# A new order of all steps, and a new choice of GpSimd's, in a fused recurrent-attention and two-MLP kernel

## The chip, the core and the metric

One core of a Trainium2 chip runs the whole program. TensorE does matrix products (its granted clock has two levels, 1.2 and 2.4 GHz), VectorE and ScalarE elementwise work and reductions, GpSimd (POOL in the profile) elementwise work on SBUF only, SyncE (SP) issues all transfers. The metric is the device time of one execution in microseconds.

## The reference

Three computations in a row, on 4 batches of 768 tokens with 8 heads of 40:

```python
for t in range(S):                       # gated recurrent attention
    m_new = np.maximum(f_gate[:, :, t] + m, i_gate[:, :, t])
    f_stab = np.exp(f_gate[:, :, t] + m - m_new)
    i_stab = np.exp(i_gate[:, :, t] - m_new)
    C = f_stab * C + i_stab * (v_t outer k_t)
    n = f_stab * n + i_stab * k_t
    y[:, :, t] = sigmoid(o_t) * (C q_t) / np.maximum(np.abs(n . q_t), 1.0)
h = x @ w_in                             # first MLP, x: 3072 x 320, w_in: 320 x 1024
solu = h * softmax(h)
x = ((solu - mean) / sqrt(var + 1e-06) * g_ln) @ w_out
h = np.maximum(np.maximum(x @ w1, x @ w2), x @ w3)      # second MLP, 320 x 768 each
out = h @ w_out2
```

## The kernel before

The recurrence is computed in chunks of 128 tokens, 6 chunks for each of 4 batches, so there are 24 tiles t = 0 to 23; the second MLP works on pairs of tiles, g = 0 to 11. All products are made to near float32 precision by splitting an operand into a high part (rounded by ScalarE) and a low part (operand less high part, by VectorE or GpSimd) and adding the products of the parts.

Every piece of work is a generator that issues a few instructions and yields. The names of the generators, with the lines that the prediction touches:

- G: the gates' scans and exponentials; step Ga is a subtraction over 768 elements. B: small loads.
- L*key*: the weight loads, one transfer of 640 KB a piece (L249). D*n*: decoding of piece n (in0 is D0 and D1, in1 D2 and D3, out0 to out3 D4 to D7, m0_0 to m2_2 D8 to D16, last0 to last2 D17 to D19): ScalarE, then VectorE's L263, L264 and L266, GpSimd's addition at L270, and the split into high and low part: 512 columns at L285, the remaining columns in 64-row blocks at L298; out weights at L308.
- Q, W, V, S, I, T, Y: one attention tile. W is the decay matrix (load, GpSimd's mask at L375, for t of 8 and more a subtraction at L398 over 1,024 elements a partition, then an exponential); V loads values and keys and scales the keys (L423, 320 elements); S the scores (L434); I the part of earlier chunks (a multiplication at L449 for t under 6); T the state (a decay at L472, 336 elements); Y the output.
- X: the tile's normalization and gate (L543 to L545 on VectorE, then Xg at L547, Xm at L549 and the split Xs, 384 elements each). A: the first MLP (products L571, L620).
- U, P, F: the second MLP: products (L655), the maximum (L669) with a split of its result in three parts (L285, 512 elements), and the output product (L686).

The order is written out by hand in the string ORDER: each word names a generator and runs its next step, `*n` runs n of them, and `~z` lets the step's products be preceded by z warm-up products (L149, of a constant, their result overwritten). Each engine executes its own instructions in this order; semaphores hold an instruction until its operands and its buffer are free. SP's queue holds all transfers in the same order.

Two strings choose the engine of the elementwise steps that could run on either: a step that asks `on_pool` goes to VectorE unless POOL names it (the D splits, W, Xm, Xs), a step that asks `on_vector` goes to GpSimd unless VECTOR names it (Ga, Gb, V, I, T, Xg, P).

Of the kernel before, what the change touches and what calls it, by code (L numbers as in the profile page):

```python
# [800 lines left out]
```

## Time and profile before

| | us |
|---|---|
| runs, median of 3 (lowest, highest) | 658.84 (654.32, 661.03) |
| profiled execution, device time | 658.2 |
| its span, first to last instruction | 656.0 |
| its mean granted TensorE clock (share of 2.4 GHz) | 0.945 |
| busy TensorE, VectorE, ScalarE, GpSimd | 608.2, 511.5, 339.7, 230.3 |

Busy time is a sum over stages that differ: the weights are loaded and decoded in the first 180 us while the first attention tiles run; after that the tiles of both MLPs fill TensorE, and at the end little but products is left. The rows are to be read by stage. An engine's busy time includes time in which an instruction has begun and is held.

### The profile page before, as it was taken

How to read it: one execution, taken by the hardware profiler on the slowest of the kernel's cores; microseconds unless marked ns; L12 is line 12 of the kernel's file. 1: busy time of each engine (PE TensorE's matmuls, PEld its weight loads, DVE VectorE, ACT ScalarE, POOL GpSimd, SP SyncE). 2: the span in 40 equal slices, each digit the busy share in tenths (PEclk: the TensorE clock that was granted, in tenths of full speed). 3: DMA queues.
4: the chain of work that ended last, by engine and by line, in shares of the span. 5: the costliest groups of instructions: out<-in, count | busy, mean ns of one | idle time of the engine just before them, and what ended most of it. 6: DMA issues, size and time to landing. Idle time of an engine off the chain costs nothing.

```text
span 656.0 us, 12274 instructions
## 1 busy us (share of the span) xinstructions
PE 608.2 (93%) x4688; PEld 552.2 (84%) x4688; DVE 511.5 (78%) x860; ACT 339.7 (52%) x635; POOL 230.3 (35%) x201
## 2 busy tenths in 40 slices
...
GB/s 277 205 261 202 206 239 151 151 25 18 104 119 156 102 176 141 78 136 148 122 112 105 120 169 69 168 128 90 148 165 59 167 100 26 50 1 11 11 21 21
DMA packets 46319, 78.06 MB, mean 119 GB/s; under 512 B 5997, under 2 KB 28581, under 8 KB 46261
## 3 DMA queue, kind: packets, MB, share of 16 engines
...
## 4 chain that ended last, share of the span: by engine, by line
PE 43%; DMA 8%; DVE 6%; ACT 3%; POOL 2%; issue 2%; SPq 1%; POOLq 0%; DVEq 0%; ACTq 0%
PE pe L655 19%; PE ph L571 7%; PE po L686 6%; PE px L620 5%; DMA Wm<-rows_m 3%; DMA three<-qt 3%; PE pu L604 1%; PE py L509 1%; PE ps L431 1%; DMA xr<-ys 1%; POOL kw L423 1%; DVE tmp L669 1%; PE pi L460 1%; DVE Pr L434 1%; DMA sig<-og 1%
## 5 line engine op out<-in xcount | busy, mean ns | idle before, releaser
L655 PE MATMUL pe<-x2h,w 128*128 128x256 f32 x1080 | 167.3, 284 | 7.4 <-DVE tmp L669 7.4
L655 PEld LDWEIGHTS pe<-x2h,w 128*128 128x128 f32 x1080 | 143.5, 189 | 11.7 <-issue 5.8
L655 PE MATMUL pe<-x2l,w 128*128 128x256 f32 x648 | 111.8, 281 | 0.0
L655 PEld LDWEIGHTS pe<-x2l,w 128*128 128x128 f32 x648 | 92.0, 189 | 0.0
L285 POOL TENSOR_TENSOR h<-tmp,h 128x512 fp32r<-128x512 f32 x33 | 43.5, 1317 | 130.7 <-ACT h L283 130.7
L669 DVE TENSOR_TENSOR tmp<-pe,tmp 128x512 f32<-128x512 f32 x72 | 49.4, 686 | 48.6 <-PE pe L655 41.1
L571 PE MATMUL ph<-w,xh 128*128 128x512 f32 x240 | 71.5, 432 | 4.2 <-ACT xh L283 4.2
L686 PE MATMUL po<-w,h 128*128 128x320 f32 x432 | 67.9, 310 | 0.0
L620 PE MATMUL px<-w,uh 128*128 128x320 f32 x384 | 65.4, 312 | 0.0
L686 PEld LDWEIGHTS po<-w,h 128*128 128x128 f32 x432 | 64.1, 188 | 0.5
L620 PEld LDWEIGHTS px<-w,uh 128*128 128x128 f32 x384 | 58.9, 191 | 0.3
L571 PEld LDWEIGHTS ph<-w,xh 128*128 128x128 f32 x240 | 46.4, 208 | 13.1 <-ACT xh L283 4.6
L594 POOL TENSOR_TENSOR st<-st,nhalf 128x1 f32<-128x1 f32 x24 | 18.7, 777 | 97.9 <-DVE st L592 97.9
L375 POOL TENSOR_SCALAR_AFFINE_SELECT Wm<-Wm 128x1024 f32<-128x1024 f32 x24 | 27.8, 1159 | 66.4 <-DMA Wm<-rows_m 53.7
L509 PE MATMUL py<-Pr,V 128*42 128x128 f32 x384 | 35.4, 303 | 13.1 <-DVE Pr L434 13.1
L360 ACT CAST qst<-three 120x512 fp32r<-120x512 f32 x36 | 22.4, 622 | 47.4 <-DMA three<-qt 47.4
L578 ACT ACTIVATE e<-ph,st 128x1024 f32<-128x1024 f32 x24 | 26.8, 1115 | 35.6 <-DVE st L575 20.6
L571 PE MATMUL ph<-w,xl 128*128 128x512 f32 x144 | 42.9, 408 | 0.0
L509 PEld LDWEIGHTS py<-Pr,V 128*42 128x42 f32 x384 | 21.1, 126 | 23.1 <-DVE Pr L434 15.3
L283 ACT CAST h<-tmp 128x512 fp32r<-128x512 f32 x36 | 22.2, 618 | 35.0 <-DVE tmp L669 34.6
L270 POOL TENSOR_TENSOR stA<-stA,raw 128x640 int32<-128x640 int32 x20 | 34.7, 1735 | 13.5 <-DVE raw L266 13.3
L620 PE MATMUL px<-w,ul 128*128 128x320 f32 x192 | 36.6, 312 | 0.9 <-DVE ul L285 0.9
...
## 6 DMA issues: line engine op xcount, KB each, us to landing
...
```

The source lines that it names most:

```text
L270: pt(out=i32(A), in0=i32(A), in1=i32(low), op=ALU.add)
L283: nc.scalar.copy(out=hi, in_=x)
L285: sub(out=lo, in0=x, in1=f(hi), op=ALU.subtract)
L360: nc.scalar.copy(out=x[:, h4], in_=three[i])
L375: nc.gpsimd.affine_select(out=W, in_=W, pattern=[[0, H], [1, P]], compare_op=ALU.is_ge, fill=-NEG, base=0, channel_multiplier=-1)
L509: mm(py[half(hh, VW), i], lhsT=at[t, "V"][:, hh * 4 + i], rhs=at[t, "P", hh][:, i], start=True, stop=(qg is None))
L571: mm(out_n, lhsT=a, rhs=x, start=(i == 0), stop=(i == len(passes) - 1))
L578: nc.scalar.activation(out=e, in_=ph, func=AF.Exp, bias=s(0), accum_out=s(2))
L620: mm(px, lhsT=a, rhs=x, start=(i == 0), stop=(i == len(passes) - 1))
L655: mm(pe[:, j], lhsT=a, rhs=x, start=(i == 0), stop=(i == len(passes) - 1))
L669: tt(out=tmp, in0=pe, in1=tmp, op=ALU.max)
L686: mm(po[o], lhsT=h2[:, a, m, o * P:o * P + P], rhs=made[f"last{m // 2}"][:, 0, x * WC + m % 2 * DM:][:, 0:DM], start=(m0 == 0 and i == 0), ...
```

## The change

The ORDER string is new throughout; each generator is run for as many steps as before. Most products keep their place on TensorE to within a few. Warm-up products are asked for in twenty places (205 in all) instead of ten (132). One list POOL now names every elementwise step that GpSimd does, part by part for the splits of weights (`m0_1.0`, with an `l` behind it for the 64-row rest) and of the second MLP's maximum (`P1.0`); a step that it does not name runs on VectorE. What the steps compute, the tiles and their buffers stay. Of ORDER only the first part is shown.

```diff
-POOL = "D12 D15 D16 D17 D6 D7 D8 W2 W3 W4 W5 W6 X1m X2m X3s X4s X5s"
-VECTOR = "I1 P2 T3 V0 V3 X4g X5g"
+POOL = """
+Gb I4 P1.0 P1.2 P10.1 P11.1 P11.2 P2.1 P2.2 P3.0 P4.0 P4.1 P4.2 P5.0 P5.1 P6.1 P7.1 P7.2 P8.1 P8.2 P9.1 P9.2 T10 T15
+T16 T19 T20 T21 T22 T4 T8 V10 V13 V14 V16 V18 V19 V20 V22 V9 W10 W11 W12 W13 W14 W16 W17 W18 W20 W21 W22 W8 X10g X10m
+X10s X11m X12g X12m X12s X13s X14g X14m X14s X15g X15m X15s X16g X16m X16s X17g X17m X17s X18m X18s X19m X19s X1g X20s
+X21g X21s X22m X22s X23m X2g X2m X3g X4s X5g X5m X5s X6g X6m X7g X7m X7s X8g X8m X8s X9g X9m X9s m0_1.0 m0_2.0 m1_2.0
+m2_2.0l
+"""
 ORDER = """
-G Lin0*2 G Lin1 G~14 G*2 W0 D0 W0*2 Lin1 G D0 W0 D1 V0 G W0 D1 B G*2 D0 G B V1 G W0 D0 Q0 D1 D0 Lout0 D1 G D2 D1 G~52
-B G*2 D2 W1 V0 D3 T0~8 G D2 G*2 T0 S0.0~5 D2 V1 S0.1 S0.0 D1 Lout1 D2 D3 D1 Q1 S0.1 Y0 D1 D3 Lout2 D1*2 D3 D4 W1 G I1
-D1 Y0 Lout3 D3 W1 Y0 D4 S1.0~7 D4 W1 D1 Y0 D1 O0 D3 D4 D5 S1.1 T1 S1.0 D5 I1 V2 D4 T1 W2 S1.1 Y1 T1 D4 D3*2 X0 D3*2 W3
-D3 D6 D3 D5 O0 Lm0_0 D3 V2 D4 T2*2 X0 Y1 V3 X0 Y1 D6 Y1 T2 W2 I2 D7 X0 Q2 D5 W3 X0 D7 X0 Lm0_1 A0~10 D6 W2 D8 D6 D8
-Lm0_2 V3 W3 W2 D7 A0 D7 X1 D8 I2 W3 S2.0 Lm1_0 A0 S2.1 Lm1_1 D5 S2.0 A0 S2.1 Y2~9 X1*2 Q3 D5 D6 W4 A0 Y2 T3*2 Y2 X1 I3
-D5 A0 V4 D7 T3 Y2 X1 A0 D6 Lm1_2 X1 A1~20 A0 D6 A0 D7 A0 W4 D9 Lm2_0 S3.0 D7 D9 I3 S3.1 D10 S3.0 A0 X2 D10 S3.1 A0
-Lm2_1 D8 D11 Y3 V4 D9 A0 D11 W4 A0 Q4 A0 D9 A1 Y3 I4 Y3 A0 T4 V5 W4 X2 Y3 X2 T4 W5 A0 D8 T4 A1 O1 X2 D8 D10 I4 Lm2_2
-X2 A1 S4.0 X2 D10 S4.1 A0 A1 X3 A0 D8*2 Q5 A0 S4.0 A2~2 A1 A0 D8 Llast0 S4.1 O1 D9 A1 A2 D11 W6 W5 A1 X3 Y4 D9 A1
-Llast1 D12 X3 A1 D12 A2 W5 A1 Y4 I5 A1 Y4 S5.0 V6 A1 X3 A1*2 D10 S5.1 Y4 X3 A1 Llast2 W5 A1 D9 X3 D11 D12 D9 D10 S5.0
-A2 S5.1 X4 I5 Y5 D9 W7 A1 A2 D13*2 D10 D11 A2 Q6 A2 D12 D10 A2 X4 A2 D11 V7 D12 A1 Y5 I7 A2 Y5 A3 A1 Y5 V6 D10 D12 A1
-W6 D14 D11 D14 X4 D11 D13 Q6 T6 A2 T6 A2 X5 X4 U0 T6 T7 D11 A2 T6*2 D13 D15 A2 D12 A2 T6 U0 P0 A2 D15 D14 D12 A2 P0
-D14 D12 D15 D13 D17 D15 D17 Q6 A3 D14 A2 D17 D13 Q6 D13*2 A2 D14 U0 A3 A2 X4*2 A2 A3 U0 P0 W6 D13 P0 A3 D16 U0 D16 D14
...
+G Lin0*2 Lout0 G G~12 W0 G*5 G~5 G*2 D0*3 D1 Lin1 W0*2 G G~13 G*3 Q0 S0.1~12 W0 W1 G*2 D0 B D1*3 D2 V0 Lout1 D4 W0*2
+S0.1 G D0 D2*2 B D1 V0 T0~25 D2 T0 V1 D1 Lin1 W1 D1*4 D3*2 S0.0*2 Q1 Y0~10 D2 D1*3 I1 D4 D3*2 W1*2 Lout3 V1 V2 T1 B Y0
+S1.1*2 Lout2 D3 S1.0*2 Y0*2 D4*2 V2 O0 D4 D3 X0 D6 T1~6 T1 W3 Lm0_0 I1 Q2 Y1~7 D3*7 D4*2 W2 D5*2 S2.1~16 D5 Lm0_2 I2
+D5 T2 O0 Lm0_1 D6 X0 D7 W3 V3 X0 Y1*3 W2 D7 T2*2 X0*2 D8*2 D6*2 I2 W2*2 D8 S2.0 W3*2 X0 A0~11 Q3 A0 X1 D7*2 S2.1 Lm1_0
+D5*2 S2.0 Y2*3 V3 A0*2 D6 W4 S3.1 X1*2 V4 D5 D10*2 I3 Y2 X2 D8 T3*2 D6 X1 D7 S3.0 A0*2 I3 D7 Lm2_1 W4 A0*3 S3.0 Lm1_1
+X1*2 A1~25 W4 Q4 A1 D8 S3.1 W5 T3 D6 D9*2 D7 D8 A0 A0~5 A0 D9 X2*2 D12 Y3 D8*2 V6 D8 A0*5 W4 X2 D11*2 O1 X2 W5 I4 Y3*3
+X3 A1*2 S4.0 V4 X2 A0 D9 T4*2 D10*2 O1 S4.1 Lm1_2 A0*2 D9 S4.0 I4 Q5 A1*2 A2~10 A2 A1 D9 T4 S4.1 W6 Y4 I5 X3*2 A1*2 A0
+X3*2 A1*3 D11 V5 X3 D12 A2 Y4 A1 Lm2_0 A1*3 A1~4 Llast2 Y4*2 X4 D9*2 W5*2 D12 D9 D13 S5.0 D13 D11 D10*2 I5 A2 Llast1
+D12*3 S5.0 S5.1*2 Y5~6 I7 W7 D11 A2*3 A3 X4 A1*2 D10*2 A2 D13 A3 X4 V6 Llast0 D10 X4 A1*2 T6 D14*2 A2*2 D12*3 A2~7 A2
+V7 Y5 D15 W6 T6*3 T7 T6 D11*2 D13 D15 D14 U0*2 P0 A2*5 D13*2 D15 Lm2_2 U0 D14 D11*2 A2 V7 D14 P0 U0 D17 D15 D17*2 T6
+Y5 P0 U0~5 Q6 X4*2 D13*2 A3 Q6*9 A3 A2 S6.0 A2 P0 D15 W6 Y5 D14 A3*2 D13 D16*2 D17 D14 A4~9 A4 P0*2 D14 A2 D17 A3*3
...
-    def on_pool(name):
+    def pick(name):
-    def on_vector(name):
-        return tt if name in VECTOR.split() else pt
-        on_vector("Ga")(out=gr, in0=gi, in1=Mend.to_broadcast([BH, NC, P]), op=ALU.subtract)
+        pick("Ga")(out=gr, in0=gi, in1=Mend.to_broadcast([BH, NC, P]), op=ALU.subtract)
-        on_vector("Gb")(out=gf, in0=mp.unsqueeze(2).to_broadcast([BH, NC, P]), in1=gM, op=ALU.subtract)
+        pick("Gb")(out=gf, in0=mp.unsqueeze(2).to_broadcast([BH, NC, P]), in1=gM, op=ALU.subtract)
-    def decode(key, i, n, sub):
+    def decode(key, i, n, name):
-            yield from split_weight(key, halves[key, j], w[:, j], sub)
+            yield from split_weight(key, halves[key, j], w[:, j], f"{key}.{j}")
-    def split(hi, lo, x, sub):
+    def split(hi, lo, x, name):
-        sub(out=lo, in0=x, in1=f(hi), op=ALU.subtract)
-    def split_weight(key, A, w, sub):
+        pick(name)(out=lo, in0=x, in1=f(hi), op=ALU.subtract)
+    def split_weight(key, A, w, name):
-            yield from split(w[:, 0:512], w[:, 512:1024], A[:, 0:512], sub)
+            yield from split(w[:, 0:512], w[:, 512:1024], A[:, 0:512], name)
-                sub(out=w[low, to], in0=A[high, 512:640], in1=f(w[high, to]), op=ALU.subtract)
+                pick(name + "l")(out=w[low, to], in0=A[high, 512:640], in1=f(w[high, to]), op=ALU.subtract)
-            yield from split(w[:, 0:WC], w[:, WC:2 * WC], A, sub)
+            yield from split(w[:, 0:WC], w[:, WC:2 * WC], A, name)
-                on_pool(f"W{t}")(out=W, in0=W, in1=a_t, op=ALU.subtract)
+                pick(f"W{t}")(out=W, in0=W, in1=a_t, op=ALU.subtract)
-            on_vector(f"V{t}")(out=kw, in0=kw, in1=wT[:, c, b * H:(b + 1) * H].unsqueeze(2).to_broadcast([P, H, D]), op=ALU.mult)
+            pick(f"V{t}")(out=kw, in0=kw, in1=wT[:, c, b * H:(b + 1) * H].unsqueeze(2).to_broadcast([P, H, D]), op=ALU.mult)
-            on_vector(f"I{t}")(out=q, in0=q, in1=at[t, "qk"][0], op=ALU.mult)
+            pick(f"I{t}")(out=q, in0=q, in1=at[t, "qk"][0], op=ALU.mult)
-            on_vector(f"T{t}")(out=C, in0=Cs[t], in1=decb[:, b * H:(b + 1) * H, c:c + 1].to_broadcast([D, H, VW]), op=ALU.mult)
+            pick(f"T{t}")(out=C, in0=Cs[t], in1=decb[:, b * H:(b + 1) * H, c:c + 1].to_broadcast([D, H, VW]), op=ALU.mult)
-        on_vector(f"X{t}g")(out=xr, in0=xr, in1=sig[t // 3][:, t % 3], op=ALU.mult)
-        on_pool(f"X{t}m")(out=xr, in0=xr, in1=nq.unsqueeze(1).to_broadcast([P, 3, P]), op=ALU.mult)
+        pick(f"X{t}g")(out=xr, in0=xr, in1=sig[t // 3][:, t % 3], op=ALU.mult)
+        pick(f"X{t}m")(out=xr, in0=xr, in1=nq.unsqueeze(1).to_broadcast([P, 3, P]), op=ALU.mult)
-        yield from split(xh, xl, xr, on_pool(f"X{t}s"))
+        yield from split(xh, xl, xr, f"X{t}s")
-            yield from split(uh[:, sl], ul[:, sl], pu, tt)
+            yield from split(uh[:, sl], ul[:, sl], pu, "")
-        yield from split(x2t[g2][0][:, :, sl], x2t[g2][1][:, :, sl], pq, tt)
+        yield from split(x2t[g2][0][:, :, sl], x2t[g2][1][:, :, sl], pq, "")
-            yield from split(h2[:, 0, ms2], h2[:, 1, ms2], tmp, on_vector(f"P{g}"))
+            yield from split(h2[:, 0, ms2], h2[:, 1, ms2], tmp, f"P{g}.{m}")
-            procs[name] = decode(key, i, len(src), on_pool(name))
+            procs[name] = decode(key, i, len(src), name)
```

## Rows read from the trace of the kernel before

**Rows 1.** Busy us (count) by window: PE, PEld, DVE, ACT, POOL; granted clock, DMA, GB/s
```profile
0.00:60.00 60.00, 45.75 (x293) 35.24 (x293) 55.37 (x76) 37.28 (x72) 29.56 (x26) 0.72 0.76 249
60.00:120.00 60.00, 49.04 (x333) 33.60 (x334) 52.70 (x88) 38.64 (x77) 31.24 (x24) 0.80 0.62 190
120.00:180.00 60.00, 50.90 (x366) 45.74 (x366) 58.55 (x85) 43.47 (x88) 38.68 (x34) 0.91 0.21 63
180.00:240.00 60.00, 55.99 (x445) 52.64 (x444) 52.76 (x92) 27.91 (x54) 23.62 (x19) 0.97 0.50 144
240.00:540.00 300.00, 293.76 (x2395) 275.81 (x2394) 245.00 (x432) 157.37 (x280) 88.67 (x82) 1.00 0.43 123
540.00:656.00 116.00, 112.75 (x865) 109.15 (x863) 47.12 (x92) 35.03 (x69) 18.48 (x17) 1.00 0.06 20
```

**Rows 2.** Timeline at 42 us: VectorE, then GpSimd (start, length in us)
```profile
42.31 3.90 DVE L543 SCALAR_TENSOR_TENSOR nq<-nq 128x128 f32<-128x128 f32 x1
42.25 0.76 POOL L472 TENSOR_TENSOR C<-C,decb 40x336 f32<-40x336 f32 x1 [4.64 <-PE py L512]
42.97 1.01 POOL L547 TENSOR_TENSOR xr<-xr,sig 128x384 f32<-128x384 f32 x1
43.92 2.14 POOL L375 TENSOR_SCALAR_AFFINE_SELECT Wm<-Wm 128x1024 f32<-128x1024 f32 x2
```

**Rows 3.** Lines of VectorE in the first 180 us (busy us, mean ns)
```profile
L264 DVE TENSOR_SCALAR stA<-stA 128x640 int32<-128x640 int32 x20 | 21.3, 1065 | 0.7
L266 DVE SCALAR_TENSOR_TENSOR raw<-raw 128x640 int32<-128x640 int32 x20 | 21.7, 1083 | 0.1
L543 DVE SCALAR_TENSOR_TENSOR nq<-nq 128x128 f32<-128x128 f32 x6 | 8.1, 1351 | 0.0
L298 DVE TENSOR_TENSOR w<-stA,w 64x128 fp32r<-64x128 f32 x18 | 10.3, 571 | 0.8 <-ACT w L295 0.3
L423 DVE TENSOR_TENSOR kw<-kw,wT 128x320 f32<-128x320 f32 x2 | 4.8, 2421 | 0.0
```

**Rows 4.** The same lines' durations, ns: shortest, median, longest (first 180 us)
```profile
L264 DVE TENSOR_SCALAR stA<-stA x20: 493/882/1773, 11.2 to 172.9; 128x640 int32<-128x640 int32 x20
L266 DVE SCALAR_TENSOR_TENSOR raw<-raw x20: 808/816/3015, 12.8 to 174.1; 128x640 int32<-128x640 int32 x20
L543 DVE SCALAR_TENSOR_TENSOR nq<-nq x6: 280/364/3898, 42.3 to 160.6; 128x128 f32<-128x128 f32 x6
L298 DVE TENSOR_TENSOR w<-stA,w x18: 284/288/1621, 26.5 to 154.0; 64x128 fp32r<-64x128 f32 x18
L423 DVE TENSOR_TENSOR kw<-kw,wT x2: 473/2421/4369, 16.6 to 53.6; 128x320 f32<-128x320 f32 x2
```

**Rows 5.** Prices by line of moved steps; last row: shortest, median, longest
```profile
L285 POOL TENSOR_TENSOR h<-tmp,h 128x512 fp32r<-128x512 f32 x33 | 43.5, 1317 | 130.7 <-ACT h L283 130.7
L285 POOL TENSOR_TENSOR xl<-xr,xh 128x384 fp32r<-128x384 f32 x3 | 3.1, 1037 | 8.3 <-DMA gb<-rows_g 5.3 <-ACT xh L283 3.0
L449 POOL TENSOR_TENSOR gb<-gb,q 40x1024 f32<-40x1024 f32 x4 | 10.7, 2663 | 4.3 <-DMA q<-qt 4.3
L398 DVE TENSOR_TENSOR Wm<-Wm,aT 128x1024 f32<-128x1024 f32 x16 | 19.5, 1216 | 15.6 <-POOL Wm L375 15.6
L285 DVE TENSOR_TENSOR h<-tmp,h 128x512 fp32r<-128x512 f32 x3 | 2.1, 688 | 0.0
L285 DVE TENSOR_TENSOR xl<-xr,xh 128x384 fp32r<-128x384 f32 x21 | 11.6, 554 | 3.2 <-ACT xh L283 3.2
L423 POOL TENSOR_TENSOR kw<-kw,wT x6: 722/1112/1307, 20.5 to 176.5; 128x320 f32<-128x320 f32 x6
```

**Rows 6.** Timeline at 224 us: GpSimd, and TensorE behind it
```profile
224.71 3.89 POOL L423 TENSOR_TENSOR kw<-kw,wT 128x320 f32<-128x320 f32 x1
228.65 0.51 PE L480 MATMUL pc<-V,kw 128*40 128x42 f32 x16 [3.17 <-POOL kw L423]
```

**Rows 7.** Timeline of TensorE at 42 us: ten warm-up products
```profile
42.76 2.31 PE L149 MATMUL ph<-ident 128*128 128x256 bf16 x10
```

More of the change, by code (lines that the diff above doesn't have):

```diff
@@ new lines @@
+A5*2 D19 P0 U1 Q7 D18*2 V8 T8 P0*2 D19*2 F0 Q7*5 Y6 T8 T9 O2 A4*2 X6 A4*2 F0 X6 I7*2 Q7*3 A4*3 F0*3 P1 A4 Q7 X6*4 W8
+I7 T8 I7 A4*2 F0 P1 S7.0 T8*3 A5*2 S7.0 S7.1*2 Q8 A5 U1 W9 A4*3 W8*2 P1 A5*5 Y7 V9 P1*2 Y7 U1 P1 U1*2 P1 Q8*4 I8 A5*2
+V9 Q8*3 W9 U1 W8 Y7*2 X7 T9 A5*3 T9 S8.0 Q8*2 A5 T10 A5 P1 S8.0 W9 S8.1*2 P1*3 X7 I8*4 Q9 T9*4 U1*2 P1 A5*4 Q9*9 Y8
+V10 Y8 V10 P1 I9 U2 A6*3 X7*4 W10*2 A6 U2 Y8*2 X8 P1*2 I9*4 T10*6 A6*3 F1*2 A6*3 W9 S9.1*2 S9.0*2 Q10 A7*2 X8 W11 F1
+W10 A6*5 W10 Y9*2 V12 Q10 A6*2 X8*4 A7 V12 A7*2 F1 A6*2 Q10*8 I10 A8 F1 W11 P2 S10.0*2 W11 A7*3 I10 P2 O3*2 U2 Y9
```

74 lines of the change are left out of this document (29 added, 45 removed).

## The prediction

> **What bounds the kernel now.** I read the busy times by stage first [rows 1]. From 240 to 540 us TensorE is busy 293.8 of 300 us at its upper clock level (2.4 GHz, granted clock 1.00), and from 540 to 656 us 112.8 of 116: there TensorE's own work sets the time, and a reader should see that little is left to win, 6.2 us of idle in the long middle. The first 180 us are another kernel: TensorE is busy 45.8, 49.0 and 50.9 of 60 us, its granted clock is 0.72, 0.80 and 0.91 (so 33.6 + 24 + 10.8 = 68 us at the lower level, 1.2 GHz), and VectorE is busy 55.4 + 52.7 + 58.6 = 166.6 of 180 us. VectorE bounds this stage; it idles only 13.4 us.
>
> Is that VectorE work or waiting? I went to the timeline of a place where a VectorE step was slow [rows 2]. A step of L543, 128x128, took 3.90 us; GpSimd ran four steps back to back from 42.25 to 46.06 us, and the VectorE step ended 0.15 us after the last. So a "busy" VectorE can be one that is held while GpSimd works. Setting the mean of a line in the first 180 us [rows 3] against the shortest of the same instruction [rows 4] gives what was lost: L264 20 x (1.065 - 0.493) = 11.4, L266 20 x (1.083 - 0.808) = 5.5, L543 6 x (1.351 - 0.280) = 6.4, L298 18 x (0.571 - 0.284) = 5.2, L423 2 x (2.421 - 0.473) = 3.9: 32.4 us in five lines, a floor. GpSimd was busy 29.6 + 31.2 + 38.7 = 99.5 us meanwhile [rows 1], so each us of GpSimd cost VectorE about 0.33 us.
>
> It goes the other way too. At 224.71 us a GpSimd step of L423 took 3.89 us (0.722 undisturbed [rows 5]) and TensorE sat 3.17 us waiting for it [rows 6]; the granted clock of 180 to 240 us is 0.97 [rows 1].
>
> **The change, part by part.** (a) *VectorE's own work in the first stage, up to the last product of U1.* From GpSimd to VectorE come four weight splits of 512 (m0_0, m1_1, m2_1, m2_2) at 0.688, one of 640 at 0.86, six 64-row rests at 0.284, Ga at 0.75 of 1.216, I2, I3 and I5 at 1.216 (VectorE's price for 1,024 elements a partition), V1, V2, V4, V6, V7, V8 and T1, T2, T7 at 0.473 (336 elements against V's 320), P0's three and P1.1 at 0.688, X0g, X1m and X3s at 0.554: 2.75 + 0.86 + 1.70 + 0.91 + 3.65 + 4.26 + 2.75 + 1.66 = 18.5 us. From VectorE go three splits (m0_1, m0_2, m1_2), five X steps and W8: 2.06 + 2.77 + 1.22 = 6.1 us. Net **+12.5 us** [rows 4, 5]. Counting at the same prices all VectorE steps listed ahead of U2's first product in both orders gives +12.8, so the order itself moves little there.
>
> (b) *What GpSimd no longer holds.* The same steps at GpSimd's prices (1.317 a split or P, 2.663 an I, 0.722 a V or T, 1.037 an X [rows 5]; rests and Ga at the same ratio of 1.9) take 34.7 us away, and 3 x 1.317 + 5 x 1.037 + 2.63 (W8) = 11.8 come: GpSimd falls by 22.9 us, from 99.5 to 76.6. In proportion VectorE gets back 22.9 x 0.33 = 7.6 us. But the long losses came from runs of steps [rows 2], and a run shortens in length as well as in number: with the square of the load the loss of 32.4 falls by 1 - (76.6/99.5)^2 = 41%, **-13.4 us**. I take this, as the row at 42 us is nearest to it. The ends are 0 and -22.9 (every us given back). So (a) and (b) together are -0.9: moving the steps is nearly free in this stage, neither the gain nor the loss that the counts alone suggest.
>
> The Trainium skill, page "SBUF — State Buffer", section "SBUF: two separate sides", says the port pair that VectorE and GpSimd share is an exclusive lock held for the whole instruction. Read so, a VectorE step would wait for one GpSimd instruction at most; the row at 42 us shows four waited out, 3.9 us against 0.28, so here the measurement goes further than the page. By the page's rule (b) would be the proportional -7.6 and the sum below 656.2.
>
> (c) *Warm-up products and the clock.* The order asks for 205 instead of 132, in twenty places instead of ten. Raising 68 us of lower level helps only where TensorE was what VectorE waited for, and VectorE idles 13.4 us in the whole stage [rows 1]: ends 0 and -13.4, I take **-6**, since the waits are shared with ScalarE and the loads. (d) *Their price.* Of the 73 additional ones 22 stand ahead of A2, where TensorE waits anyway (five at U11 go), and 56 from A2's first product on; ten of 256 columns took 2.31 us at the lower level [rows 7], so 0.23 each there and half of it at the upper: 6.5 to 12.9 us. TensorE's idle time from 60 to 180 us, 11.0 + 9.1 [rows 1], hides most; I take **+4**, with ends 0 and 12.9 where the cover is gone.
>
> (e) *The stall at 224 us.* V8 goes to VectorE, where it takes its turn: **-3** of the 3.17 us [rows 6]; ends 0 and -5, with the clock regained (0.03 of 60 us is 1.8 us). What is late next is the chain through L362 on VectorE that held it.
>
> (f) *From U2 on.* Eleven W subtractions, 27 X steps and two P splits leave VectorE (13.4 + 15.0 + 1.4), eleven P, seven Xg, six V and T come (7.6 + 3.9 + 2.8): -15.4 us. GpSimd gets 28.9 + 28.0 + 2.6 and gives 26.1: +33.4 us. A W step has no GpSimd row; the nearest are I's 2.663 (as many elements) and twice a split, 2.63. VectorE is not the bound here, so of the 6.2 us idle TensorE I take **-2**; ends -6 and the first rival.
>
> (g) *Loads.* The order shifts SP's queue: the second piece of in1 waits behind B, V0, V1 and the gate rows; V6 stands ahead of V5; Lm2_2 is last of the weights. VectorE, 55.4 of 60 us busy, covers this: 0. Uncovered, one 640 KB load at the 249 GB/s of 0 to 60 us is 2.6 us [rows 1].
>
> **Sum:** 12.5 - 13.4 - 6 + 4 - 3 - 2 = -7.9 us, against the profiled execution's 658.2 us (span 656.0 and 2.2 around it): **650.3 us**. The runs shown have a median of 658.84, so this is 1.3% faster.
>
> **The rivals.** *GpSimd's runs reach into the steady stage (slower).* A mask (1.07 us [rows 2]) and now its subtraction of 2.63 on the same engine are a run of 3.7 us, and three X steps one of 3.1; a VectorE step that meets them waits, with the max steps and score products that feed TensorE queued behind. VectorE has 55 us idle in 240 to 540 [rows 1], thirteen tokens, 4.2 us a token, 5.2 with the relief of (f). Held longer than 5.2 us a token, the rest falls on TensorE: both runs in full are 6.8, 1.6 us over, 12 times 19 us: 650.3 + 2 + 19 = **671**. Against it: nearly all of the 33 P splits on GpSimd [rows 5] run after 180 us already, and TensorE still idles only 2%.
>
> *The change does little (no change).* Losses fall only in proportion (12.5 - 7.6), the clock gives nothing because VectorE was never waiting for it, the products cost 4, the stall goes, (f) is nothing: +5.9, less 3: **661**. For it: VectorE idle is small; against it: run lengths.
>
> *All shared waiting goes (much faster).* (b) at -22.9, (c) at -11, (d) +2, (e) -5, (f) -4: 12.5 - 40.9 = -28.4: **630**. For it: 32.4 is a floor; against it: the load of GpSimd is still 77 us.
>
> **How the numbers follow.** My forecast 0.38, with its own range 641 to 660; no change 0.26; much faster 0.18; slower 0.18. About 1% is what a measurement of this kernel can tell from no change, so faster is below 652. Of my forecast five eighths lie there (0.24), and with the much faster case and a little of the second rival that is 0.44; the rest of my forecast (0.14) and 0.20 of the second give same 0.34; the slower case and the tail of the second 0.22. The range 632 to 670 leaves out half of the two outer cases, 0.18.
>
> **What would show it.** In the changed profile's first 180 us: mean of L264 from 1.07 to about 0.8 us and GpSimd near 77 us busy (b); granted clock above 0.72, 0.80 and 0.91 (c); the same TensorE work reached some 5 us sooner; no wait of TensorE for L423 near 220 us (e); TensorE idle at most 6 us in 240 to 540 (f). I am wrong if L264 and L543 are as slow as before, if VectorE's steps lengthen beside the W subtractions, or if TensorE waits for xh or for a weight.

## The result, and the profile after

The changed kernel takes 661.73 us (656.73 to 665.76), beside 656.23 us for the kernel before on the same chip: a ratio of 1.0077, 95% interval 1.0051 to 1.0103. It is 0.8% slower, where 1.3% faster was forecast. Its profiled execution takes 664.41 us with a span of 662.6. Lines of the changed kernel have numbers lower by 7 (L264 is L257, L655 is L648).

The stages of after, one row a window (PE, PEld, DVE, ACT, POOL busy us; granted clock, DMA share, GB/s), as [rows 1]:

```profile
0.00:60.00 60.00, 49.87 (x311) 36.90 (x313) 53.69 (x87) 37.86 (x74) 24.86 (x20) 0.81 0.80 248
60.00:120.00 60.00, 51.80 (x404) 37.87 (x405) 55.13 (x101) 40.80 (x80) 22.92 (x18) 0.91 0.55 175
120.00:180.00 60.00, 50.29 (x387) 46.05 (x386) 56.58 (x94) 40.82 (x85) 25.72 (x21) 0.97 0.26 84
180.00:240.00 60.00, 58.03 (x472) 54.08 (x471) 50.98 (x84) 31.36 (x60) 28.35 (x25) 1.00 0.50 153
240.00:540.00 300.00, 284.79 (x2297) 268.54 (x2295) 228.49 (x401) 147.19 (x263) 101.94 (x97) 0.98 0.39 117
540.00:663.00 123.00, 118.51 (x905) 114.79 (x903) 55.21 (x104) 38.89 (x78) 16.08 (x16) 0.99 0.09 28
```

The first 180 us look as forecast in GpSimd, busy 24.9 + 22.9 + 25.7 = 73.5 us (99.5 before), and in the clock of the second and third window (0.91 and 0.97 for 0.80 and 0.91). The first window's 0.81 for 0.72 is no rise. The profile counts time ahead of the trace's first clock record as the upper level; that record stands at 23.0 us in after and at 11.0 in before. TensorE's products ran at the lower level ahead of it, as the score products of after show, first up to 22 us, then from 95 to 160 us, where the granted clock is 1.00 (mean ns):

```profile
L424 PE MATMUL ps<-q,k 40*128 40x128 f32 x8 | 2.1, 437 | 0.7 <-DMA q<-qt 0.7
L424 PE MATMUL ps<-q,k 40*128 40x128 f32 x16 | 2.0, 278 | 0.0
```

With the unrecorded time counted as lower level the first window has 0.61 in after and 0.62 in before. What is new is the long middle: TensorE idles 15.2 us of 300 from 240 to 540 us, 6.2 before, and its clock is no longer 1.00.

The same stretch, all that TensorE waited for (total us, times, longest us), first of after:

```profile
PE ps L424 <- DVE kst L355: 6.9, 3, 3.6
PE ph L564 <- DVE u L576: 2.3, 2, 1.6
PE pq L625 <- ACT x L616: 2.3, 1, 2.3
PE po L679 <- DVE Pr L427: 1.6, 1, 1.6
PE pe L648 <- DVE tmp L662: 1.2, 1, 1.2
PE pu L597 <- DVE u L589: 0.8, 1, 0.8
```

and of before, where no wait is over 1.2 us:

```profile
PE pq L632 <- ACT x L623: 2.8, 4, 1.1
PE pe L655 <- DVE tmp L669: 2.6, 4, 1.2
PE ps L431 <- DVE kst L362: 0.5, 1, 0.5
PE pc L480 <- POOL kw L423: 0.4, 2, 0.2
```

After has nine waits where before has eleven, but they sum to 15.1 us (6.3 before), 12.8 of it for VectorE. The longest one in after's timeline (start, length; idle time before it and its cause in brackets):

```profile
398.44 5.97 DVE L355 SCALAR_TENSOR_TENSOR qst<-qst,part,three 120x512 fp32r<-120x512 f32 x1
397.84 0.90 POOL L491 TENSOR_TENSOR Cl<-C,cst 40x336 fp32r<-40x336 f32 x1
398.71 1.09 POOL L368 TENSOR_SCALAR_AFFINE_SELECT Wm<-Wm 128x1024 f32<-128x1024 f32 x1
399.76 1.30 POOL L278 TENSOR_TENSOR h<-tmp,h 128x512 fp32r<-128x512 f32 x1
401.02 1.89 POOL L391 TENSOR_TENSOR Wm<-Wm,aT 128x1024 f32<-128x1024 f32 x1
402.88 0.98 POOL L542 TENSOR_TENSOR xr<-xr,nq 128x384 f32<-128x384 f32 x1
404.34 0.74 DVE L355 SCALAR_TENSOR_TENSOR kst<-kst,part,three 120x512 fp32r<-120x512 f32 x1
405.13 1.00 PE L424 MATMUL ps<-qst,kst 120*128 120x128 f32 x4 [3.57 <-DVE kst L355]
```

GpSimd ran five steps back to back from 397.84 to 403.86 us: a mask and its subtraction, with a split and an X step between and behind. A VectorE step took 5.97 us beside them, until 0.55 us after the last; the next of the same kind took 0.74. (L355, L362 before, makes the two operands of the scores.) The step behind it was late for the scores, and TensorE sat 3.57 us. The granted clock behind this wait, behind the one at 378 us and behind a third that ended at 478.36 us (1.98 us long), in windows:

```profile
378.00:382.00 4.00, 4.00 (x20) 4.00 (x20) 3.96 (x8) 2.10 (x4) 0.20 (x1) 0.58 0.40 86
405.00:409.00 4.00, 3.87 (x14) 3.35 (x15) 2.56 (x5) 0.97 (x2) 0.00 (x0) 0.57 0.39 123
480.00:484.00 4.00, 4.00 (x19) 4.00 (x20) 1.40 (x4) 0.97 (x2) 0.00 (x0) 0.57 0.42 129
```

A mean near 0.58 is mostly the lower level (1.2 GHz). In each of these three windows that is 0.42 or 0.43 of 4 us, so some 1.7 us of lost work on top of the wait.

Where the time goes is told by TensorE's progress: the first product of a pair of tiles g in the second MLP, us later (+) or sooner (-) than in before, worked out from the traces of the runs below:

```
                              U0     U2     U4     U5     U6     U8    last
after                       -4.9   -7.9   -5.1   -4.4   +3.7   +6.1   +6.5
b_choicea (old order)       -8.8   -6.9   -9.4   -9.9  -10.7   -6.0   -6.0
ba_newc (new order from U2) -7.3   -5.3   -4.4   -3.7   -0.3   +5.7   +6.6
ab_newc (new order to U2)   -8.4   -5.8   -4.5   -3.8   -4.1   +1.7   +1.7
a_lessp                     -2.1   -5.1   -4.7   -5.1   -4.8   -3.9   -3.4
```

After is 7.9 us ahead at U2 (211 us) and loses 14.4 us from there to the end. Some 5 us of that lead are no gain: sixteen products of the first MLP and four score products that before makes ahead of U2 stand behind it in after (16 x 0.30 + 4 x 0.14 us, the mean busy time of one in before). At U4 both have made the same products, and there after is 5.1 us ahead. From U4 to the end (after, then before):

```profile
311.00:659.30 348.30, 335.22 (x2641) 319.16 (x2639) 228.35 (x407) 150.28 (x276) 92.65 (x90) 0.99 0.29 86
316.10:652.80 336.70, 331.74 (x2645) 314.68 (x2643) 230.71 (x415) 148.53 (x275) 87.75 (x82) 1.00 0.31 90
```

After takes 11.6 us longer here: TensorE idles 13.1 us instead of 5.0, and three times 1.7 us go to the lower clock. Of the loss 8.1 us fall between U5 and U6: that is 359 to 413 us, where the waits at 378 and 405 us lie. One caution: runs that share all their code up to U2 differ there by up to 8 us, so single entries are to be read to a few us, and verdicts rest on the ratios.

### The profile page after: what moved, and what is told of

The parts are those of the page before. It is cut to its first block, busy times and chain, and to the rows that moved or that the text cites. A ratio compares the mean times of both kernels' runs of the same rounds, so it can differ in the third digit from the quotient of the medians.

```text
span 662.6 us, 12377 instructions
## 1 busy us (share of the span) xinstructions
PE 613.3 (93%) x4761; PEld 558.2 (84%) x4761; DVE 500.1 (75%) x866; ACT 336.9 (51%) x635; POOL 219.9 (33%) x195
## 4 chain that ended last, share of the span: by engine, by line
PE 55%; DVE 22%; DMA 9%; ACT 6%; issue 4%; SPq 2%; POOL 0%; ACTq 0%; DVEq 0%; POOLq 0%
PE pe L648 22%; PE ph L564 10%; PE po L679 6%; PE px L613 6%; DMA three<-kt 3%; PE ps L424 2%; DMA three<-qt 2%; PE py L502 2%; PE pu L597 2%; DMA q<-qt 2%; DVE u L576 2%; DVE kst L355 2%; DVE st L567 2%; DVE raw L259 1%; ACT e L571 1%
## 5 line engine op out<-in xcount | busy, mean ns | idle before, releaser
L648 PE MATMUL pe<-x2h,w 128*128 128x256 f32 x1080 | 166.7, 284 | 4.5 <-DVE tmp L662 3.0
L648 PEld LDWEIGHTS pe<-x2h,w 128*128 128x128 f32 x1080 | 143.8, 189 | 7.8 <-issue 2.7
L648 PE MATMUL pe<-x2l,w 128*128 128x256 f32 x648 | 111.4, 280 | 0.0
L648 PEld LDWEIGHTS pe<-x2l,w 128*128 128x128 f32 x648 | 91.7, 188 | 0.0
L679 PE MATMUL po<-w,h 128*128 128x320 f32 x432 | 70.3, 317 | 1.6 <-DVE Pr L427 1.6
L564 PE MATMUL ph<-w,xh 128*128 128x512 f32 x240 | 67.7, 413 | 3.8 <-DVE u L576 3.8
L679 PEld LDWEIGHTS po<-w,h 128*128 128x128 f32 x432 | 66.1, 194 | 2.4 <-DVE Pr L427 1.8
L564 PEld LDWEIGHTS ph<-w,xh 128*128 128x128 f32 x240 | 44.5, 197 | 13.3 <-DVE u L576 2.9
L278 POOL TENSOR_TENSOR h<-tmp,h 128x512 fp32r<-128x512 f32 x20 | 27.4, 1368 | 78.6 <-ACT h L276 65.7
L355 DVE SCALAR_TENSOR_TENSOR qst<-qst,part,three 120x512 fp32r<-120x512 f32 x36 | 37.6, 1044 | 15.3 <-ACT qst L353 12.2
L276 ACT CAST uh<-pu 128x512 fp32r<-128x512 f32 x48 | 26.0, 588 | 35.2 <-PE pu L597 35.1
L587 POOL TENSOR_TENSOR st<-st,nhalf 128x1 f32<-128x1 f32 x24 | 14.2, 594 | 87.3 <-DVE st L585 87.2
L567 DVE TENSOR_REDUCE st<-ph 128x1 f32<-128x512 f32 x48 | 30.7, 681 | 15.7 <-PE ph L564 15.7
L142 PEld LDWEIGHTS <-ident 128*128 128x128 bf16 x205 | 24.3, 127 | 17.1 <-issue 9.3
```

Source lines behind the costliest of these rows:

```text
L276: nc.scalar.copy(out=hi, in_=x)
L278: pick(name)(out=lo, in0=x, in1=f(hi), op=ALU.subtract)
L355: nc.vector.scalar_tensor_tensor(out=x[:, h4], in0=f(x[:, h4]), scalar=part[:, i:i + 1], in1=three[i], op0=ALU.mult, op1=ALU.add)
L564: mm(out_n, lhsT=a, rhs=x, start=(i == 0), stop=(i == len(passes) - 1))
L567: nc.vector.tensor_reduce(out=s(n), in_=ph[:, n * 512:(n + 1) * 512], axis=AX.X, op=ALU.max, negate=True)
L648: mm(pe[:, j], lhsT=a, rhs=x, start=(i == 0), stop=(i == len(passes) - 1))
```

## The experiments

Theory 1: the gain is lost again by the late choice, GpSimd's runs of mask and subtraction above all (the prediction's slower rival). Theory 2: it is lost by the order itself, which the prediction counted at nothing. Ratios are to the kernel before of the same call, with their 95% interval.

### Choice of engines, and order

**b_choicea**: the new choice, in the order and with the warm-ups of before.

```diff
-POOL = "D12 D15 D16 D17 D6 D7 D8 W2 W3 W4 W5 W6 X1m X2m X3s X4s X5s"
-VECTOR = "I1 P2 T3 V0 V3 X4g X5g"
+POOL = """
+Gb I4 P1.0 P1.2 P10.1 P11.1 P11.2 P2.1 P2.2 P3.0 P4.0 P4.1 P4.2 P5.0 P5.1 P6.1 P7.1 P7.2 P8.1 P8.2 P9.1 P9.2 T10 T15
...
```

> The order and the warm-ups of before; only the choice of engines is the changed one, everywhere. Theory 1: the late runs cost as much as in the changed kernel (about +12) and the early relief gives some of its 6 to 8 us: 658 to 668 us, with L362 (the same step as L355) held for several us at least once. Theory 2: the choice alone does no harm, 650 to 657 us.

Measured: 650.27 us, 0.9857 (0.9811 to 0.9902): faster than both kernels. Its first three windows, its middle, and its L264 (here L269):

```profile
0.00:60.00 60.00, 46.61 (x317) 35.01 (x317) 55.47 (x93) 39.34 (x76) 24.57 (x20) 0.74 0.78 256
60.00:120.00 60.00, 51.00 (x372) 38.73 (x369) 55.76 (x99) 43.10 (x85) 24.68 (x19) 0.83 0.66 200
120.00:180.00 60.00, 47.66 (x352) 43.06 (x351) 58.97 (x93) 40.79 (x82) 29.32 (x23) 0.97 0.20 60
240.00:540.00 300.00, 290.86 (x2353) 272.71 (x2352) 234.79 (x404) 147.66 (x266) 111.34 (x98) 0.99 0.42 121
L269 DVE TENSOR_SCALAR stA<-stA 128x640 int32<-128x640 int32 x20 | 16.0, 798 | 0.7
```

GpSimd is busy 78.6 us in the first 180 (76.6 forecast) and the mean of L264 is 0.80 us (about 0.8 forecast). In the middle GpSimd does 111.3 us, more than in after, and TensorE idles only 9.1. So the late choice does no harm that this measurement can tell in the order of before.

**splice_u2, ab_newc, ba_newc**: one order ahead of U2's first product, the other behind it. splice_u2 has the order, warm-ups and choice of after, then those of before; ab_newc the same with the new choice throughout; ba_newc the new choice throughout, the order of before, then that of after.

```diff
 ORDER = """
-G Lin0*2 Lout0 G G~12 W0 G*5 G~5 G*2 D0*3 D1 Lin1 W0*2 G G~13 G*3 Q0 S0.1~12 W0 W1 G*2 D0 B D1*3 D2 V0 Lout1 D4 W0*2
+G Lin0*2 G Lin1 G~14 G*2 W0 D0 W0*2 Lin1 G D0 W0 D1 V0 G W0 D1 B G*2 D0 G B V1 G W0 D0 Q0 D1 D0 Lout0 D1 G D2 D1 G~52
...
```

This is the beginning of ba_newc's order against that of after; behind U2's first product its words stand as in after. In ab_newc and splice_u2 it is the other way round.

> The changed kernel's order, warm-ups and choice up to U2's first product, then the order and the choice of before for what is left. Theories 1 and 2 alike: 648 to 651 us, because U2 starts at 211.4 us instead of 219.3 and what follows is as before. Theory 3 (the early gain is only borrowed: steps were put off, and the late stage pays for them whatever its order): 655 to 658 us.

> The changed choice of engines everywhere; the changed order and its warm-ups up to U2's first product, then the order of before. Theory A (the choice gains about 8 us in the first 120 us, the changed order of the late steps loses about 12 between 300 and 510 us): 649 to 654 us, with TensorE busy 290 or more of 300 us from 240 to 540 us. Theory B (the changed order already harms in the early stage, by leaving later work unprepared): 657 to 662 us.

> The changed choice of engines everywhere; the order and warm-ups of before up to U2's first product, then the changed order. Theory A: 659 to 664 us, the loss of the late order in full, TensorE busy about 285 of 300 us from 240 to 540 us. Theory B: 649 to 654 us.

Measured: splice_u2 1.0009 (0.9984 to 1.0034); ab_newc 0.9995 (0.9963 to 1.0027); ba_newc 1.0118 (1.0078 to 1.0158). All three have the good choice ahead of U2, and none keeps b_choicea's gain: the new order costs 1.4% where it stands early (with its warm-ups) and 2.6% where it stands late. The two don't add: after, with both, is 2.2% behind b_choicea. For splice_u2 (659.25 us) theories 1 and 2 both missed, and theory 3 came nearest; ab_newc (657.88) is where theory B had it; ba_newc (665.75) went past theory A's 664. So both parts of the new order cost. Theories 3 and B both say that its early part puts steps off which are paid for later. The progress table fits that: ab_newc is 5.8 us ahead at U2, b_choicea 6.9, with the same products made and the same order behind, and by U4 they are 4.9 us apart, 7.7 at the end. It doesn't prove it, as the seam between two orders that were not made for each other may cost something as well.

**b_to_u6**: as ba_newc, but the order changes at U6. Against b_choicea it differs only from there on:

```diff
 ORDER = """
...
-P5 S17.1 Y16 S17.0 P5 A14 U6 P5 V18 S17.1 A14*2 W19 U6 Y16 A14 Y16 A14 Y16 A14 V18 I17 A15 I17 W19 T18 X16 I17 T18 A14
...
```

> The new choice of engines with the order and warm-ups of before up to U6's first product, then the order of after. The same with the change of order at U2 was 1.0118, and the order of before to the end 0.9857. If the late order loses place by place (in the profiles two thirds of the loss are made by U6): 0.989 to 0.995. If it is lost after U6 or at the joint, wherever it stands: 1.003 to 1.012.

Measured: 0.9892 (0.9831 to 0.9953). The late order's loss is made on the way, most of it ahead of U6; from U6 on the new order and the seam there cost together 0.35%, which is within the noise of the two runs.

### Which part of the choice

**b_attn**: the kernel before with only I2, I3, I5, V1, V2, V4, V6, V7, V8, T1 and T2 moved to VectorE. Its list against the list that says the same as before's two strings:

```diff
-V1 V2 V4 V6 V7 V8 V9 V10 V12 V13 V14 V15 V16 V18 V19 V20 V21 V22 I2 I3 I4 I5 T1 T2 T4 T7 T8 T9 T10 ...
+V9 V10 V12 V13 V14 V15 V16 V18 V19 V20 V21 V22 I4 T4 T7 T8 T9 T10 ...
```

**b_early_newc**: b_choicea with the choice of before from U2 on. **a_lateb**: after, likewise with the choice of before from U2 on (W8 stays on GpSimd in both, the other W go to VectorE). Their lists begin

```diff
-Gb I4 P1.0 P1.2 P10.1 P11.1 P11.2 P2.1 P2.2 P3.0 P4.0 P4.1 P4.2 P5.0 P5.1 P6.1 P7.1 P7.2 P8.1 P8.2 P9.1 P9.2 T10 T15
+m0_1.0 m0_2.0 m1_2.0 m2_2.0l Gb X1g X2g X2m X3g I4 T4 X4s X5g X5m X5s X6g X6m X7g X7m X7s W8 T8 X8g V9 X9g V10 T10
...
```

(b_early_newc; a_lateb has no X7m and X7s.)

> The kernel before with eleven early attention steps alone moved from GpSimd to VectorE: I2, I3, I5, V1, V2, V4, V6, V7, V8, T1, T2. By the prediction's prices VectorE's own work grows by 3.65 + 8 x 0.473 = 7.4 us and GpSimd's falls by 8.0 + 8 x 0.722 = 13.8. Theory P (long GpSimd steps hold VectorE for longer than VectorE itself needs for them): 649 to 654 us, most of the gain of the whole choice (8.5 us), and the mean of L264 from 1.07 to 0.9 us or less. Theory Q (the gain comes from the weight splits and the late steps): 656 to 662 us.

> The order and warm-ups of before; the changed choice of engines for the steps ahead of U2's first product only, the choice of before for later ones. Theory A (the gain of the choice is made in the first 120 us): 648 to 652 us, and the W subtractions on GpSimd are worth nothing in this order. Theory C (the late choice matters, VectorE's relief in the steady stage): 653 to 658 us.

> The changed order and warm-ups; the changed choice of engines for all steps ahead of U2's first product, the choice of before for all later ones. Theory 1 (runs on GpSimd in the steady stage): 649 to 654 us, since the early gain of 6 to 8 us stays and the late loss goes. Theory 2 (order): 660 to 664 us. If only W matters within theory 1, this and the kernel with W alone put back are alike within 2 us.

Measured: b_attn 0.9936 (0.9912 to 0.996), about half the gain from eleven steps; b_early_newc 0.9888 (0.9843 to 0.9933), nearly all of it; a_lateb 1.0425 (1.038 to 1.047). The same late choice is worth 0.3% in the old order, within the noise, and 3.5% in the new one. Theory 1 as first put falls: without the late choice the new order is far worse. Theory 2 (as changed, 660 to 664 us) missed a_lateb's 687.33 us as well. In b_attn the other sign that was expected, a mean of L264 of 0.9 us or less, did not come (it is L268 there; 1.07 us before):

```profile
L268 DVE TENSOR_SCALAR stA<-stA 128x640 int32<-128x640 int32 x20 | 23.0, 1148 | 0.7
```

The mean of one line does not tell the gain; VectorE's busy time up to U2 does better (the rows under (a) and (b) below).

### Warm-ups

**b_newc_warm**: b_choicea with the 205 warm-ups at after's steps. **b_newc_nowarm**: b_choicea with none. **a_oldwarm**: after with the 132 of before.

```diff
-G Lin0*2 Lout0 G G~12 W0 G*5 G~5 G*2 D0*3 D1 Lin1 W0*2 G G~13 G*3 Q0 S0.1~12 W0 W1 G*2 D0 B D1*3 D2 V0 Lout1 D4 W0*2
+G Lin0*2 Lout0 G G~14 W0 G*8 D0*3 D1 Lin1 W0*2 G G~52 G*3 Q0 S0.1 W0 W1 G*2 D0 B D1*3 D2 V0 Lout1 D4 W0*2 S0.1 G D0
...
```

This is a_oldwarm against after: only the `~z` differ, the steps stay. In the same way b_newc_warm asks for `G~12` where b_choicea has `G~14`, and b_newc_nowarm has no `~z` at all.

> The order of before with the changed choice of engines (650.3 us with the warm-ups of before), and the changed kernel's 205 warm-up products ahead of the same steps as there. If the warm-ups do nothing where VectorE bounds the stage: 648 to 652 us, with a higher granted clock in the first 180 us. If they gain: 643 to 647 us. If they cost TensorE time: 653 to 657 us.

> The order of before with the changed choice, and no warm-up product at all. If warm-ups only cost where VectorE bounds the stage: 646 to 650 us, at a lower granted clock in the first 120 us. If the 132 of before are worth having: 653 to 660 us.

> The changed order and choice with the 132 warm-up products of before, ahead of the same steps as there, in place of the 205. If the additional warm-ups cost what they cost in the order of before (5 us): 655 to 659 us. If they are worth their time here, where the granted clock of the first 180 us rose to 0.81, 0.91 and 0.97: 663 to 668 us.

Measured: b_newc_warm 0.9943 (0.9904 to 0.9981), b_newc_nowarm 0.9887 (0.9845 to 0.9928), a_oldwarm 1.0152 (1.0109 to 1.0195). In the old order the 73 additional products cost 0.9% and none at all does as well as 132 within the noise (651.96 us, between the two ranges that were expected); in the new order the 73 are worth 0.7%. b_newc_nowarm's first windows, and then b_newc_warm's:

```profile
0.00:60.00 60.00, 33.14 (x202) 24.64 (x204) 55.41 (x93) 39.42 (x76) 24.58 (x20) 0.98 0.79 256
60.00:120.00 60.00, 53.57 (x329) 38.34 (x328) 48.06 (x90) 39.96 (x79) 23.28 (x18) 0.70 0.64 194
0.00:60.00 60.00, 44.58 (x305) 34.62 (x305) 56.39 (x88) 37.72 (x73) 24.39 (x20) 0.83 0.77 251
60.00:120.00 60.00, 51.12 (x400) 37.22 (x401) 55.25 (x96) 42.20 (x84) 23.24 (x18) 0.89 0.66 199
```

The 0.98 of b_newc_nowarm is again time without a clock record, here up to 50.7 us. Its output products of attention, up to 50 us and from 99 to 112 us (granted clock 1.00), show the lower level:

```profile
L513 PE MATMUL py<-Pr,V 128*42 128x128 f32 x32 | 5.8, 425 | 3.5 <-DVE Pr L438 3.5
L513 PE MATMUL py<-Pr,V 128*42 128x128 f32 x32 | 3.4, 289 | 0.0
```

With that time counted as lower level the first window has 0.56 without warm-ups, 0.64 with 132 (b_choicea) and 0.69 with 205, and the second 0.70, 0.83 and 0.89. The clock rises with the number of warm-ups, and the time doesn't follow: none and 132 end within 0.3% of each other, and 205 is the slowest (its profiled execution, 662.07 us, is one of its longest). So a higher clock in the first stage is not by itself worth its price.

### Why VectorE is late in the new order

**a_wvec**: after, with the twelve W subtractions that it has on GpSimd back on VectorE. **a_repair**: after, with six products that waited moved one or two TensorE steps later (one of the six places is shown).

```diff
-T16 T19 T20 T21 T22 T4 T8 V10 V13 V14 V16 V18 V19 V20 V22 V9 W10 W11 W12 W13 W14 W16 W17 W18 W20 W21 W22 W8 X10g X10m
+T16 T19 T20 T21 T22 T4 T8 V10 V13 V14 V16 V18 V19 V20 V22 V9 X10g X10m X10s X11m X12g X12m X12s X13s X14g X14m X14s
...
```

```diff
-Q11 P2*2 U2 Q11*5 S11.0 Q11*3 A7*2 P2*3 U2 W11 S11.0
+Q11 P2*2 U2 Q11*8 A7*2 P2*3 U2 S11.0 W11 S11.0
...
```

> The changed kernel with one thing put back: the twelve W subtractions (L391, 1.90 us each on GpSimd, 1.22 on VectorE) run on VectorE again; order, warm-ups and all other choices as changed. Theory 1 (runs: at 398.44 us a step of L355 took 5.97 us instead of 0.75 because GpSimd ran Cl, mask, P, W and Xm back to back; such runs in the steady stage hold VectorE and then TensorE): most of the 12 us lost between 300 and 510 us come back, 651 to 656 us, mean of L355 from 1.04 and 0.85 back to about 0.8 us. Theory 2 (order: the new order of the late steps loses the time, whichever engine does them): 660 to 664 us, as changed.

> The changed kernel with six places of its late order mended and nothing else: products that TensorE began by waiting for VectorE (S11.0, A10's first, A12's first, S17.0, A14's transposes, S20.0; waits of 1.31, 1.60, 0.71, 3.57, 0.77 and 1.98 us, 9.9 together) stand one or two TensorE steps later, so that TensorE does ready work while VectorE finishes. Theory O (the late order sets products too close behind the VectorE steps that they wait for): 652 to 657 us, with TensorE busy about 291 of 300 us from 240 to 540 us. Theory V (VectorE itself is too late in this order, so the waits only move to the next product): 659 to 664 us.

Measured: a_wvec 1.0178 (1.0134 to 1.0223), worse by 1.0% than after, which both theories missed (671.78 us). a_repair 1.0073 (1.005 to 1.0097), no change. Its waits from 240 to 540 us begin with

```profile
PE pc L473 <- POOL kw L416: 4.4, 2, 3.6
PE pq L625 <- ACT x L616: 2.8, 2, 2.5
PE ps L424 <- DVE kst L355: 2.3, 3, 1.0
```

The total is no less, 14.4 us beside 15.1: it moved from the scores to the state's products. So the loss does not lie in the place of these six products. A guess that remains is that VectorE and GpSimd have no room in this order. The next runs take work away, in either order.

**a_lessv, b_lessv** leave out two VectorE steps a tile (tiles 8 to 23, 16 x 1.22 = 19.5 us), in after and in b_choicea; **a_lessp, b_lessp** leave out the W subtractions of tiles 9 to 23; **a_lessvp** both, in after. The expectations of the W runs take all fifteen subtractions for GpSimd's. In the new choice only eleven of them are (11 x 1.9 = 21 us); W9, W15, W19 and W23 are VectorE's (4 x 1.22 = 4.9 us) and go too.

```diff
-        ts(out=nq, in0=nq, scalar1=1.0, scalar2=None, op0=ALU.max)
-        nc.vector.reciprocal(out=nq, in_=nq)
+        if t < 8:
+            ts(out=nq, in0=nq, scalar1=1.0, scalar2=None, op0=ALU.max)
+            nc.vector.reciprocal(out=nq, in_=nq)
```

```diff
-                pick(f"W{t}")(out=W, in0=W, in1=a_t, op=ALU.subtract)
+                if t == NA:
+                    pick(f"W{t}")(out=W, in0=W, in1=a_t, op=ALU.subtract)
```

> The kernel after, with two of VectorE's own steps (the maximum and the reciprocal of nq, 0.42 and 0.95 us) left out for tokens 8 to 23, so the scores are not normed there: 16 x 1.37 = 22 us less VectorE work in the steady stage. The kernel after is at 1.0077. Theory V (in the late part of the new order VectorE's own load makes its results late for TensorE): at least half of the 12 us comes back, 0.988 to 0.997. Theory H (VectorE is late because runs of GpSimd steps hold it): little, 1.001 to 1.008. Theory P (TensorE's products stand too close whatever the others do): 1.005 to 1.010.

> The new choice of engines in the order and with the warm-ups of before (0.9857), with the same two VectorE steps left out for tokens 8 to 23 as in a_lessv: 22 us less VectorE work. Theory V says that VectorE is late only in the new order's steps: 0.982 to 0.987, a gain of at most 0.4%. If less VectorE work helps here as much as in the new order (0.970 to 0.980), its load says nothing of the order.

> The kernel after, with GpSimd's W subtractions left out for tokens 9 to 23 (the decay is not subtracted there): 15 x 1.9 = 28 us less GpSimd work in the steady stage, no VectorE step less. Theory H: the runs of mask and W are halved, at least half of the 12 us comes back, 0.988 to 0.997. Theory V: GpSimd's share is small, 1.002 to 1.008. Theory P: 1.005 to 1.010.

> The new choice of engines in the order and with the warm-ups of before (0.9857), with GpSimd's W subtractions left out for tokens 9 to 23 as in a_lessp (there 28 us less GpSimd work gave 1.2%). If the order of before has room for these steps, as it had for the 22 us of VectorE work left out in b_lessv (0.9859): 0.982 to 0.987. If runs of GpSimd steps hold VectorE in either order at the same price, the new order is not what makes them dear: 0.970 to 0.977.

> The kernel after with both left out: the two VectorE steps of a_lessv (alone 0.9977) and the W subtractions of a_lessp (alone 0.9953); after itself is at 1.0077. If both act on the same waits (VectorE's room in the steady stage, whichever engine fills it), the second adds little: 0.990 to 0.996. If they act on separate waits, the gains add: 0.983 to 0.988. In either case it should not go below the order of before with the same left out (about 0.985).

Measured:

| left out | in after (1.0077) | in b_choicea (0.9857) |
|---|---|---|
| VectorE's two steps | 0.9977 (0.9943 to 1.0011) | 0.9859 (0.9804 to 0.9914) |
| W subtractions (eleven GpSimd, four VectorE) | 0.9953 (0.9911 to 0.9995) | 0.9874 (0.9841 to 0.9907) |
| both | 0.9949 (0.9921 to 0.9977) | |

In the old order neither gives anything that can be told from noise. In the new order each gives about 1%, and both together no more than the better one alone, as expected if the two act on the same waits. a_lessp is where theory H had it and theory V had not; a_lessv lies just outside V's range and outside H's; theory P missed both. The W runs are no clean test of GpSimd, because of the four VectorE steps: at a_lessv's rate (1.0% for 19.5 us) these would be worth 0.25% of the 1.2%. In a_lessv's one profile (659.75 us, its median is 655.90) the late loss is still there (the kernel is 13.0 us ahead at U2 and 1.9 behind at the end), so only its ratio speaks for it. a_lessp's profile fits the mechanism; its middle, and the VectorE steps that were held at 398 us in after:

```profile
240.00:540.00 300.00, 291.78 (x2379) 275.29 (x2378) 225.32 (x407) 153.07 (x275) 87.38 (x89) 1.00 0.41 122
395.27 0.99 DVE L355 SCALAR_TENSOR_TENSOR qst<-qst,part,three 120x512 fp32r<-120x512 f32 x1
396.56 1.41 DVE L355 SCALAR_TENSOR_TENSOR kst<-kst,part,three 120x512 fp32r<-120x512 f32 x1 [0.30 <-ACT kst L353]
397.90 1.50 DVE L355 SCALAR_TENSOR_TENSOR qst<-qst,part,three 120x512 fp32r<-120x512 f32 x1
399.32 0.74 DVE L355 SCALAR_TENSOR_TENSOR kst<-kst,part,three 120x512 fp32r<-120x512 f32 x1
```

With the subtraction out of the run, no step here is over 1.50 us, TensorE idles 8.2 us in the middle instead of 15.2, its clock is 1.00, and it loses 1.7 us from U2 to the end instead of 14.4.

Three things stay open. Why the early part of the new order costs 1.4% was not taken apart beyond the warm-ups; that it puts steps off is likely and not shown. With both kinds of work left out after is at 0.9949, still about 0.8% behind the old order with either left out. And no run shows which words of the late order take the room away; only that the loss builds up from place to place, and that taking work off gives some of it back in this order alone.

## Why the prediction was wrong

A chain of three steps splits the result: from before to b_choicea is the choice, from there to a_oldwarm the order, from there to after the warm-ups. In us, the differences of the ratios times 658 (each is good to some 3 to 4 us):

| part | forecast | measured |
|---|---|---|
| choice of engines (a, b, e, f) | 12.5 - 13.4 - 3 - 2 = -5.9 | -0.0143: -9.4 |
| order | 0 | 1.0152 - 0.9857: +19.4 |
| warm-ups (c, d) | -6 + 4 = -2 | 1.0077 - 1.0152: -4.9 |
| sum | -7.9 | +5.1 |

Another chain would share the sum out differently: choice and order don't add, as with the late choice of before the new order costs far more (a_lateb).

**The step that failed** is the last sentence of (a), "so the order itself moves little there", together with (f), which took VectorE as "not the bound here" from U2 on. The order, counted at nothing, measured +19.4 us. Counting the steps ahead of U2 told how much work lies in a stage; it says nothing of how far each result lies ahead of the product that uses it, and it overlooked the sixteen first-MLP products that moved behind U2. The profile of before had the warning in it: from 240 to 540 us VectorE was busy 245.0 and TensorE 293.8 of 300 [rows 1], which suggests steps arranged so that VectorE is ahead (in after it was busy 228.5, less, and late). A new order had to be taken as a term with its own ends, and the 6.2 us of idle TensorE as what the old order had achieved, not as all that could be lost.

**(a) and (b)** held in the old order. Up to U2's first product (before, b_choicea, b_attn):

```profile
0.00:219.30 219.30, 184.15 (x1309) 151.03 (x1309) 200.67 (x306) 138.85 (x273) 114.00 (x96) 0.84 0.53 163
0.00:212.40 212.40, 177.67 (x1310) 147.71 (x1310) 199.21 (x332) 138.93 (x274) 89.08 (x73) 0.87 0.54 168
0.00:214.40 214.40, 179.72 (x1310) 148.29 (x1310) 196.76 (x317) 139.00 (x273) 100.94 (x85) 0.87 0.53 166
```

In b_choicea VectorE runs 26 steps more and is busy 1.5 us less (-0.9 forecast), with GpSimd down by 24.9 us (22.9 forecast): the own work moved to VectorE is given back by GpSimd's shorter presence. The rest of the 6.9 us at U2 is idle time of VectorE, 18.6 us before and 13.2 now, which the prediction had put down to the warm-ups in (c); b_choicea has those of before. (The working's 41% of 32.4 us is 13.2, not 13.4.) In after the relief of the two lines with the largest loss is smaller:

```profile
L259 DVE SCALAR_TENSOR_TENSOR raw<-raw 128x640 int32<-128x640 int32 x20 | 19.4, 969 | 0.1
L257 DVE TENSOR_SCALAR stA<-stA 128x640 int32<-128x640 int32 x20 | 18.9, 945 | 0.7
L536 DVE SCALAR_TENSOR_TENSOR nq<-nq 128x128 f32<-128x128 f32 x7 | 2.0, 280 | 0.0
```

L264 is at 0.95 us and L266 at 0.97 (1.07 and 1.08 before [rows 3]), while L543, 1.35 us before, is at its undisturbed 0.28: with less GpSimd work in after (73.5 us) than in b_choicea, how much is lost depends on which steps meet.

The Trainium skill, page "SBUF — State Buffer", section "SBUF: two separate sides", says that the port pair which the two engines share is locked for one whole instruction. The step of 5.97 us was held over four whole GpSimd steps and the end of the one before, and so the trace goes further than the page, as the row at 42 us did.

**(c) and (d)** had the right sign for the new order, -2 against -4.9, and their reason is not borne out. The 68 us at the lower level lacked the 11 us ahead of the first clock record. The clock did rise from 60 us on (0.91, 0.97 for 0.80, 0.91), and the additional products took 35.2 - 19.9 = 15.3 us of TensorE in the first 240 us, over the upper end of 12.9. But in the old order the clock rose with the warm-ups too, and there the first 132 gain nothing over none and the 73 more lose 0.9%, 6 us. Clock and price are not shown apart. What the warm-ups do for the new order is not explained by these runs.

**(e)** held: after has no wait for L423 (L416 there) from 180 to 240 us, and that window's clock is 1.00.

**(f) and the slower rival.** The rival named the place (a run of mask and subtraction in the steady stage), and the row at 398 us is that run; the VectorE steps there lengthened beside a W subtraction, one of the prediction's signs of being wrong, and taking the subtractions away gives 1.2%, 8 us. Its price of 19 us was the whole of two runs. But its condition, that the runs alone use up VectorE's room, was wrong: in the old order the same subtractions on GpSimd cost nothing (b_lessp), and in the new one it is still better to have them there than on VectorE (a_wvec). The order, which decides whether these runs cost anything, was not among its conditions. The subtraction itself was overpriced: 1.9 us on GpSimd, for an estimated 2.63.

**The second rival** (no change) was priced at 661, but its own terms give 12.5 - 7.6 + 4 - 3 = +5.9, 664: its "less 3" counts the stall a second time. That +5.9 lies next to the measured +5.1 is luck. Without the products it has the choice at +1.9, which gained 9.4, and it has no term for the order, which lost 19.4.
